# FAVOR+ attention followed by a gated MLP on one core: instruction order from an event-by-event model, tanh in place of silu, fewer DVE scalars and a second buffer for fetched weights

## Chip, core and metric

One core of one Trainium2 chip. The metric is the device time of one execution in microseconds (us); lower is better. A core has five instruction queues that run side by side, each strictly in its own order: PE (matrix multiply; its weight loads are shown as PEld), ACT (activation functions and copies), DVE (vector), POOL (a second vector engine) and SP (which here only issues DMA transfers). An instruction at the head of a queue that waits for data holds everything behind it on that queue.

## What is computed

```python
scale = D ** -0.25                                # 8 batches, 8 heads, 576 rows, D = 64
phi(x) = exp(x @ omega.T - sum(x*x)/2 - max) / sqrt(128)        # 128 features
q_p, k_p = phi(q * scale), phi(k * scale)
kv, z = k_p.T @ v, sum(k_p)                       # per batch and head
x = (q_p @ kv) / (q_p @ z + 1e-6)                 # 4608 x 512, heads side by side
g, val = x @ w_gate, x @ w_val                    # 512 x 1536 each
out = (g * sigmoid(g) * val) @ w_out              # 4608 x 512, float32
```

## The kernel before

**Attention.** The (batch, head pair, 256 rows) groups are walked in 72 steps (`NS`), two groups a step: first k groups alone, from step 6 a q group beside a k group, at the end q groups alone. Step n goes through these functions: `load` and `load_v` issue the loads of `nat` (q and k) and `v` on SP (L341, L348; `nat` has 3 buffers); `st_transpose` transposes on PE (`pt`, L383), squares on POOL (`sq`, L390) and copies to `x` on ACT (L391); `st_project` multiplies by omega (`pp`, L406); `st_max` reduces squares and maxima on DVE (L417 to L427) into a statistics tile `st`, the bias of the exponentials; `st_exp` makes the eight exponentials of the step on ACT (`ph`, L438); `k_accumulate` sums k features times v on PE (`kvacc`, L540) two steps later; `q_transpose`, `q_mult`, `q_out` and, for batches from 4 on, `q_den` and `q_norm` make x from the q features. The sums z of these later batches go through `kv_finalize`, which also transposes them on PE (L460) and writes them to DRAM, and `load_z`, which reads them back on all partitions.

**Weights.** The three weight matrices come in as 64-bit floats seen as pairs of 32-bit words. `convert_all` makes 36 pieces of 128x512 float32 out of them. One piece is: a 512 KB load (`st<-in_moe_w_...`, L232 or L237) into one of **two** staging buffers (`tag="stw"`; the trace calls this tile `st` too, but its lines tell it from the statistics), two ACT instructions (L268 and L276), three DVE instructions (L270, L272, L274), one POOL addition (L278), and a 256 KB write of the result to a scratch tensor (`wscr`, L281). The first nine pieces are also split at once into a high and a low part (`split_piece`: ACT L250, POOL L251). A staging buffer is free for the load of the piece after next when the POOL addition is done.

**MLP.** Float32 products are made of three matmuls of high and low parts. `stream` visits (512 tokens, three of the twelve weight slices): three times `g` (L657, 12 matmuls each), silu from PSUM to `sl` on ACT (L731), outstanding down projections (`o`, L666), three times `v` (L657), the product `sl` times `v` on DVE (L750), its split, and later the down projections. `g`, `v` and `o` share three PSUM buffers. The last four token tiles are done in pairs (`pair_rounds`): seven products instead of eight (`product`, L872), whose operands `make_seven` forms on DVE (L848 to L851) from weight pieces that `fetch` reads back into three `wraw` buffers (L306); there silu is in `gate` (L944).

**Order.** The Python loop at the end walks the steps and, in each, calls the functions in a fixed list (`CLOSE` while n < `EARLY`, then `GROUPED`), gives the MLP a share (`give`) and the conversion a number of ticks (`tick`) so that six pieces are due by step `EARLY` and the rest by later marks. What is traced earlier has priority. The order in which each queue finally holds its instructions is found afterwards by the library's scheduler: it plays the program through a model of the machine and gives every queue, whenever it comes free there, the ready instruction of highest priority. Silu and the exponential need different tables on ACT, and a table load stands before each change between them.

## Time and profile before

| | |
|---|---|
| three runs | 1203.81, 1209.05, 1226.72 us; median 1209.05 |
| the profiled execution | 1207.78 us; its span in the trace 1206.0 us |
| granted TensorE clock | 0.993 of full on average |
| PE idle in the span | 1206.0 - 1165.7 = 40.3 us |
| PE idle from 0 to 37 us | 9.95 us |
| PE idle from 37 to 130.3 us (attention only) | 4.25 us |
| PE idle from 130.3 to 452 us (attention and MLP) | 15.4 us |
| PE idle from 452 to 844 us | 1.3 us |
| PE idle from 844 to 876 us (first pair) | 4.5 us |

How to read it: a row of a group gives line, engine, operation, the tile written and those read, the count, then busy us, mean ns of one, and the idle time of the engine just before them with what ended it. A row of the timeline gives start us, length us, engine, line, operation and count; in square brackets stand idle time of the engine before it and what ended that. A row of the waits gives the waiting engine and line, what it waited for, total us, times, longest. Matmuls overlap, so a busy PE is not a PE at its peak: a matmul of 128x512 shows about 390 ns, but one follows the other 227 ns later.

### The profile page before, as it was taken

The numbers are of one execution on the slowest core, as the hardware profiler recorded it, in microseconds if no ns is written. First come the engines' busy times: TensorE is split into PE (matmuls) and PEld (weight loads), VectorE is DVE, ScalarE is ACT, GpSimd is POOL, SyncE is SP. The second block draws the span as 40 slices with busy tenths as digits, with TensorE's granted clock in tenths as the row PEclk, the third lists the DMA queues.
The fourth block names the chain that finished last, engine by engine and source line by source line (L and its number), as shares of the span: only waits on it lengthen the run. The fifth ranks groups of instructions, "written<-read, shape, count | busy, mean of one in ns | idle before, by whom it ended". The sixth has DMA issues, their size and how long they took to land.

```text
span 1206.0 us, 18814 instructions
## 1 busy us (share of the span) xinstructions
PE 1165.7 (97%) x6705; PEld 964.4 (80%) x6705; DVE 595.7 (49%) x1159; ACT 679.9 (56%) x1497; POOL 572.7 (47%) x500
## 2 busy tenths in 40 slices
PE   6999999999999999999999999999899999999998
PEld 5888787877887778888888787878688888888886
DVE  3687674345454644434332353373534556535544
ACT  4888977576566555556465656343454435454431
POOL 3333343334254546535445776344655543555541
PEclk9999999999999999999999999999999999999999
DMA  6555665344344423345222221334311111321103
GB/s 150 141 136 142 164 201 159 87 125 134 103 118 131 138 74 79 79 107 122 62 60 68 71 66 45 106 87 139 88 53 53 53 44 27 105 53 53 53 18 70
DMA packets 174110, 113.53 MB, mean 94 GB/s; under 512 B 125856, under 2 KB 144320, under 8 KB 174016
## 3 DMA queue, kind: packets, MB, share of 16 engines
q1 hardware_dynamic: 174016, 112.32, 34.9%
q8 instruction: 53, 0.87, 0.3%
q14 instruction: 41, 0.34, 0.1%
HBM read 87.10 MB, written 25.18 MB: 93 GB/s over the span
## 4 chain that ended last, share of the span: by engine, by line
PE 66%; DMA 4%; DVE 3%; POOL 3%; ACT 3%; issue 2%; SPq 1%; POOLq 0%; ACTq 0%; DVEq 0%
PE o L666 22%; PE a L872 10%; PE v L657 8%; PE g L657 8%; PE c L872 5%; PE pp L406 3%; PE d L872 2%; PE kvacc L540 2%; PE ptq L564 2%; PE xt L621 1%; PE pt L383 1%; POOL wlo L251 1%; DMA st<-in_moe_w_out_dram 1%; ACT ph L438 1%; DMA nat<-in_k_dram 1%
## 5 line engine op out<-in xcount | busy, mean ns | idle before, releaser
L438 ACT ACTIVATE ph<-pp,st 128x128 f32<-128x128 f32 x576 | 157.6, 389 | 17.0 <-DVE st L427 16.4
L695 DVE TENSOR_TENSOR acc<-o,acc 128x512 f32<-128x512 f32 x140 | 95.7, 685 | 104.7 <-PE o L666 104.7
L390 POOL TENSOR_TENSOR sq<-nat 128x512 f32<-128x512 f32 x72 | 75.6, 1051 | 146.0 <-DMA nat<-in_k_dram 116.9
L424 DVE TENSOR_REDUCE st<-pp 128x4 f32<-128x512 f32 x144 | 92.8, 683 | 72.5 <-PE pp L406 72.3
L251 POOL TENSOR_TENSOR wlo<-wraw,whi 128x512 fp32r<-128x512 f32 x76 | 99.9, 1324 | 55.3 <-ACT whi L250 55.1
L666 PE MATMUL o<-whi,hh 128*128 128x512 f32 x240 | 97.3, 406 | 3.1 <-ACT sl L731 3.0
L666 PE MATMUL o<-whi,hl 128*128 128x512 f32 x240 | 95.1, 396 | 1.2 <-POOL hl L754 1.2
L657 PE MATMUL g<-xh,whi 128*128 128x512 f32 x240 | 96.1, 400 | 0.0
L657 PE MATMUL v<-xh,whi 128*128 128x512 f32 x240 | 95.7, 399 | 0.2 <-DVE acc L695 0.2
L500 POOL TENSOR_TENSOR jk<-ph,zt 128x512 f32<-128x512 f32 x32 | 41.6, 1305 | 112.8 <-ACT ph L438 112.8
L666 PE MATMUL o<-wlo,hh 128*128 128x512 f32 x240 | 95.1, 396 | 0.0
L406 PE MATMUL pp<-omT,x 64*128 64x128 f32 x1152 | 92.8, 297 | 2.3 <-ACT x L391 2.2
L657 PE MATMUL g<-xh,wlo 128*128 128x512 f32 x240 | 94.0, 392 | 0.0
L657 PE MATMUL v<-xh,wlo 128*128 128x512 f32 x240 | 93.8, 391 | 0.0
L657 PE MATMUL g<-xl,whi 128*128 128x512 f32 x240 | 93.8, 391 | 0.0
L657 PE MATMUL v<-xl,whi 128*128 128x512 f32 x240 | 93.6, 390 | 0.0
L754 POOL TENSOR_TENSOR hl<-sl,hh 128x512 fp32r<-128x512 f32 x60 | 79.0, 1320 | 27.1 <-ACT hh L753 26.9
L406 PEld LDWEIGHTS pp<-omT,x 64*128 64x128 f32 x1152 | 76.0, 196 | 19.1 <-issue 11.6
L417 DVE TENSOR_REDUCE st<-sq 128x8 f32<-128x512 f32 x72 | 49.1, 681 | 85.5 <-POOL sq L390 85.4
L863 POOL TENSOR_TENSOR wlo<-s,whi 128x512 fp32r<-128x512 f32 x44 | 65.3, 1502 | 34.3 <-DVE late L969 11.8
L863 POOL TENSOR_TENSOR wlo<-wraw,whi 128x256 fp32r<-128x256 f32 (+1 forms) x44 | 45.2, 1026 | 74.9 <-ACT whi L862 74.7
L540 PE MATMUL kvacc<-v,ph 128*128 128x65 f32 x512 | 69.3, 277 | 3.4 <-ACT ph L438 3.4
(251 smaller groups left out, 2854.8 us busy)
## 6 DMA issues: line engine op xcount, KB each, us to landing
wraw<-wscr SPq DMA_DIRECT2D x120, 256.0 KB, 2.7
wscr<-wc SPq DMA_DIRECT2D x36, 256.0 KB, 2.4
out_dram<-acc SPq DMA_DIRECT2D x72, 128.0 KB, 2.3
nat<-in_k_dram SPq DMA_DIRECT2D x64, 128.0 KB, 3.1
v<-in_v_dram SPq DMA_DIRECT2D x64, 128.0 KB, 3.2
nat<-in_q_dram SPq DMA_DIRECT2D x64, 128.0 KB, 3.0
st<-in_moe_w_gate_dram SPq DMA_DIRECT2D x12, 512.0 KB, 5.2
st<-in_moe_w_val_dram SPq DMA_DIRECT2D x12, 512.0 KB, 4.6
```

Source lines behind the costliest of these rows:

```text
L251: nc.gpsimd.tensor_tensor(lo, raw, hi.bitcast(F32), op=ALU.subtract)
L390: nc.gpsimd.tensor_tensor(sq, nat, nat, op=ALU.mult)
L406: nc.tensor.matmul(pp[hh][:, i, c, :], x[r, i, c * P : (c + 1) * P], omT[r], start=True, stop=True)
L424: nc.vector.tensor_reduce(st[:, 1, :, :, hh], pp[hh], axis=AX.X, op=ALU.max, negate=True)
L438: nc.scalar.activation(ph[:, c, hh * M : (hh + 1) * M], pp[hh][:, i, c, :], AF.Exp, bias=st[:, 3, i, c, hh : hh + 1], scale=1.0,)
L540: nc.tensor.matmul(acc[:, 2 * (pr % 2) + hh, :], ph[:, c, hh * M : (hh + 1) * M], vt[:, 2 * c + j if gr is None else c, hh, :], start=firs ...
L657: nc.tensor.matmul(ps, a_[:, ws], b_[:, c, :], start=n == 0, stop=n == 3 * NC - 1)
L666: nc.tensor.matmul(ps, a_[:, ts_], b_, start=first and n == 0, stop=last and n == 2)
L695: nc.vector.tensor_tensor(a_, po, a_, op=ALU.add)
L754: nc.gpsimd.tensor_tensor(hl, h, hh.bitcast(F32), op=ALU.subtract)
L863: nc.gpsimd.tensor_tensor(lo, src_, hi.bitcast(F32), op=ALU.subtract)
L872: nc.tensor.matmul(ps, a_[:, w_], b_[:, c, :], start=start and c == 0 and m == 0, stop=c == CH - 1 and m == 2, skip_group_check=True,)
```

## The change

1. The whole kernel stands inside `tc.block(schedule_with_timeline_sim=True)`: the scheduler finds the order with a different model of the machine, an event-by-event one. No priority and no call is changed by this line.
2. `st_max` and `q_den`: sums with constants (`-SQC`, `EPS`) become reductions over a pair of columns, one of which a POOL memset has filled once. Per step that is three small reductions in place of two `scalar_tensor_tensor`; the statistics are six fixed tiles instead of six buffers of a pool.
3. `kv_finalize` no longer transposes the sums z; `z_rows` does, called first in each step's list (`GROUPED`), so one step later.
4. In `stream`, silu becomes tanh(g/2) on ACT, and (tanh + 1) times g on DVE, read from the same PSUM buffer (L750 of the changed file); the factor 0.5 goes into the product with `v`. In `gate` of the pairs, silu stays.
5. In the pairs, `fetch` for the next pair's first two weight kinds uses the five `first` buffers of the pool `win`, which are free by then, instead of the three `wraw` buffers.

```diff
+    ctx.enter_context(tc.block(schedule_with_timeline_sim=True))
     nc = tc.nc
...
-    def fetch(fs, i):
+    def fetch(fs, i, spare=None):
...
-            raw = moe.tile([P, DM], F32, name=f"wraw{f}_{i}", tag="wraw", bufs=3)
+            if spare is None:
+                raw = moe.tile([P, DM], F32, name=f"wraw{f}_{i}", tag="wraw", bufs=3)
+            else:
+                raw = spare.tile([P, DM], F32, name=f"wspare{f}_{i}", tag="first", bufs=5)
...
-        nc.vector.tensor_reduce(
-            st[:, 0].rearrange("p i c h -> p (i c h)"),
-            sq.rearrange("p i c h d -> p (i c h) d"),
-            axis=AX.X,
-            op=ALU.add,
-        )
+        nc.vector.tensor_reduce(st[:, :, 0], sq.rearrange("p i c h d -> p (i c h) d"), axis=AX.X, op=ALU.add)
+        nc.vector.tensor_reduce(st[:, :, 3], st[:, :, 0:2], axis=AX.X, op=ALU.mult)
...
-            nc.vector.tensor_reduce(st[:, 1, :, :, hh], pp[hh], axis=AX.X, op=ALU.max, negate=True)
-        s0, s1, s2, s3 = (st[:, j].rearrange("p i c h -> p (i c h)") for j in range(4))
-        nc.vector.scalar_tensor_tensor(s2, s0, SQC, s1, op0=ALU.mult, op1=ALU.add)
-        nc.vector.scalar_tensor_tensor(s3, s0, -SQC, s2, op0=ALU.mult, op1=ALU.add)
+            nc.vector.tensor_reduce(top[:, :, :, hh], pp[hh], axis=AX.X, op=ALU.max)
+        nc.vector.tensor_reduce(st[:, :, 4], st[:, :, 2:4], axis=AX.X, op=ALU.add, negate=True)
+        nc.vector.tensor_reduce(st[:, :, 5], st[:, :, 3:5], axis=AX.X, op=ALU.add)
...
+    def z_rows():
+
+        for (b, a2), raw in zraw.items():
             zp = ps_att(f"zp{b}_{a2}", [4, P])
             nc.tensor.transpose(zp, raw[:, :, D], ident)
...
-                nc.scalar.activation(sl, pg[f], AF.Silu)
+                nc.scalar.activation(sl, pg[f], AF.Tanh, scale=0.5)
+                nc.vector.scalar_tensor_tensor(sl, sl, 1.0, pg[f], op0=ALU.add, op1=ALU.mult)
...
-                nc.vector.tensor_tensor(h, pv, h, op=ALU.mult)
+                nc.vector.scalar_tensor_tensor(h, pv, 0.5, h, op0=ALU.mult, op1=ALU.mult)
...
-                        coming[i] = fetch((2 * pf2, 2 * pf2 + 1), i)
+                        coming[i] = fetch((2 * pf2, 2 * pf2 + 1), i, late_pools["win"])
...
     GROUPED = (
+        lambda n: z_rows(),
         q_out,
```

**What moves.** Three places, on the queues that the prediction is about. In the rows, the number after `ph`, `kvr` or `nat` that isn't its last is the step, the first number after `wc`, `whi` or a weight's `st` is the weight kind, and last numbers are only tile identities; `x2` is two instructions of one row.

The first is ACT at attention steps 5 and 6. Before:

```order
L391 COPY x_436<-pt_431 128x512
L438 ACTIVATE ph_5_454<-pp_5_420,st_382 128x128 x2
L438 ACTIVATE ph_5_454<-pp_5_421,st_382 128x128 x2
L438 ACTIVATE ph_5_459<-pp_5_420,st_382 128x128 x2
L438 ACTIVATE ph_5_459<-pp_5_421,st_382 128x128 x2
L391 COPY x_488<-pt_483 128x512
L454 COPY kvr_1_497<-kvacc_1_392 128x260
L268 ACTIVATE wc_0_595<-st_0_369 128x512
L438 ACTIVATE ph_6_509<-pp_6_471,st_437 128x128 x2
```

Now, the same engine from the last exponentials of step 4 on:

```order
L442 ACTIVATE ph_4_435<-pp_4_384,st_124 128x128 x2
L269 ACTIVATE wc_1_1183<-st_1_896 128x512
L277 ACTIVATE st_1_896<-st_1_896 128x512
L269 ACTIVATE wc_1_1473<-st_1_1179 128x512
L277 ACTIVATE st_1_1179<-st_1_1179 128x512
L251 CAST whi_1_1181<-wc_1_1183 128x512
L398 COPY x_460<-pt_455 128x512
L442 ACTIVATE ph_5_478<-pp_5_444,st_125 128x128 x2
L442 ACTIVATE ph_5_478<-pp_5_445,st_125 128x128 x2
L442 ACTIVATE ph_5_483<-pp_5_444,st_125 128x128 x2
L442 ACTIVATE ph_5_483<-pp_5_445,st_125 128x128 x2
L269 ACTIVATE wc_2_1885<-st_2_1469 128x512
```

Two pieces of the conversion (`wc`) now stand between the exponentials of one step and those of the next. Counting the first instructions of a piece (L268, now L269) ahead of each step's exponentials: before, 2 are ahead of step 4, 3 of step 9, 5 of step 15, 8 of step 24 and 19 of step 34; now 4 are ahead of step 4, then 6, 8, 10, 12 and 14 of steps 5 to 9, 19 of step 15, and still 19 of step 34. From step 36 on PE has the same counts of MLP and attention matmuls ahead of nearly every step as before.

The second is SP, which issues the loads. Before, at the loads of the fourth piece (`st_1_591`):

```order
L341 DMA nat_519<-in_q_dram 128x4x64
L341 DMA nat_519<-in_k_dram 128x4x64
L341 DMA v_101<-in_v_dram 128x4x64
L281 DMA wscr<-wc_0_373 128x512
L341 DMA nat_577<-in_q_dram 128x4x64
L341 DMA nat_577<-in_k_dram 128x4x64
L341 DMA v_102<-in_v_dram 128x4x64
L232 DMA st_1_591<-in_moe_w_val_dram 128x4x256
```

Now, at the loads of the sixth, seventh and eighth piece:

```order
L233 DMA st_1_1179<-in_moe_w_val_dram 128x4x256
L345 DMA v_102<-in_v_dram 128x4x64
L282 DMA wscr<-wc_1_1183 128x512
L238 DMA st_2_1469<-in_moe_w_out_dram 128x1024
L345 DMA nat_488<-in_q_dram 128x4x64
L345 DMA nat_488<-in_k_dram 128x4x64
L345 DMA v_103<-in_v_dram 128x4x64
L282 DMA wscr<-wc_1_1473 128x512
L345 DMA v_104<-in_v_dram 128x4x64
L238 DMA st_2_1881<-in_moe_w_out_dram 128x1024
```

Here a load of a piece and a write of a piece stand between the loads of every two attention steps, and each of them waits for the conversion of an earlier piece. Before, the loads of several steps stood between two of them.

The third is ACT at a visit of the MLP. Before, around the silus of one visit:

```order
L753 CAST hh_8_5358<-sl_8_5096 128x512
L731 ACT_TABLE_LOAD
L731 ACTIVATE sl_9_5473<-g_9_5368 128x512
L731 ACTIVATE sl_10_5475<-g_10_5382 128x512
L731 ACTIVATE sl_11_5477<-g_11_5395 128x512
L636 COPY xo_7_5_5418<-xt_7_5415 128x256
L566 COPY qt_8_5436<-ptq_8_5431 128x512
L391 COPY x_5468<-pt_5463 128x512
L438 ACT_TABLE_LOAD
```

Now:

```order
L772 CAST hh_8_5400<-sl_8_5133 128x512
L749 ACTIVATE sl_9_5514<-g_9_5410 128x512
L749 ACTIVATE sl_10_5517<-g_10_5424 128x512
L749 ACTIVATE sl_11_5520<-g_11_5437 128x512
L654 COPY xo_7_5_5460<-xt_7_5457 128x256
L584 COPY qt_8_5478<-ptq_8_5473 128x512
L442 ACTIVATE ph_52_5490<-pp_52_5463,st_124 128x128 x2
```

The two table loads around them are gone. In the whole program 58 of them stood on ACT and 2 are left: one at the start, and one at the first `gate` of the pairs.

## Prediction

> **What bounds the kernel now.** The page comes first, for the share of each engine.

> ```profile
> span 1206.0 us, 18814 instructions
> PE 1165.7 (97%) x6705; PEld 964.4 (80%) x6705; DVE 595.7 (49%) x1159; ACT 679.9 (56%) x1497; POOL 572.7 (47%) x500
> ```

> PE is the bound, idle for 40.3 us in all. What a new order can gain lies in those and in stretches where PE is busy but slow; what it can lose is open, so the next view is the table by stretches.

> ```profile
> 0.00:37.00 37.00, 27.05 (x156) 24.21 (x157) 15.19 (x33) 17.10 (x47) 14.53 (x31) 1.00 0.55 135
> 37.00:57.40 20.40, 19.25 (x197) 17.74 (x196) 14.32 (x33) 17.36 (x54) 7.34 (x7) 1.00 0.67 167
> 57.40:130.30 72.90, 69.80 (x663) 62.75 (x662) 56.59 (x152) 61.50 (x186) 26.20 (x24) 1.00 0.58 144
> 130.30:223.00 92.70, 88.61 (x615) 74.45 (x614) 51.84 (x127) 70.66 (x169) 32.17 (x29) 1.00 0.56 157
> 223.00:452.00 229.00, 217.67 (x1319) 179.42 (x1318) 113.45 (x221) 140.10 (x306) 102.35 (x86) 0.99 0.42 118
> 452.00:844.00 392.00, 390.66 (x2230) 315.81 (x2229) 160.33 (x307) 213.74 (x461) 205.85 (x180) 1.00 0.32 84
> 844.00:876.00 32.00, 27.47 (x106) 21.44 (x106) 18.65 (x30) 15.34 (x28) 18.95 (x15) 0.89 0.33 93
> ```

> The columns are the stretch, its length, busy us of PE, PEld, DVE, ACT and POOL, the granted clock, the DMA share and GB/s. From 37 to 130 us there is attention alone, and no engine is far from full: ACT 78.9 of 93.3 us, DVE 70.9, PE 89.1. From 130 us the MLP fills PE. From 452 us on PE waits for almost nothing, so an order has little to win there except at the first pair (844 to 876). The timeline then gives the pace of the attention, by the exponentials of steps 4, 5 and 9:

> ```profile
> 37.04 2.18 ACT L438 ACTIVATE ph<-pp,st 128x128 f32<-128x128 f32 x8 [0.83 <-DVE st L427]
> 40.81 2.18 ACT L438 ACTIVATE ph<-pp,st 128x128 f32<-128x128 f32 x8 [0.48 <-DVE st L427]
> ...
> 57.41 2.18 ACT L438 ACTIVATE ph<-pp,st 128x128 f32<-128x128 f32 x8
> ```

> Steps 4 to 9 take 57.4 - 37.0 = 20.4 us, 4.1 a step.

> **The change, part by part.** *The order of the conversion* is the largest term. The new order of ACT has two pieces ahead of the exponentials of each of the steps 5 to 9 (4 ahead of step 4, 14 ahead of step 9). ACT works in its order, so step n can't start its exponentials before two more pieces have been loaded. Loads go through two staging buffers, and piece k + 2 can only be loaded when piece k has gone through all of this:

> ```profile
> st<-in_moe_w_gate_dram SPq DMA_DIRECT2D x12, 512.0 KB, 5.2
> st<-in_moe_w_val_dram SPq DMA_DIRECT2D x12, 512.0 KB, 4.6
> st<-in_moe_w_out_dram SPq DMA_DIRECT2D x12, 512.0 KB, 3.8
> L268 ACT ACTIVATE wc<-st 128x512 f32<-128x512 f32 x36 | 24.3, 676 | 20.2 <-POOL wlo L251 6.0 <-DMA st<-in_moe_w_gate_dram 5.9 <-DMA st<-in_moe_w_out_dram 5.8
> L270 DVE TENSOR_SCALAR wc<-wc 128x512 f32<-128x512 f32 x36 | 23.4, 649 | 22.6 <-ACT wc L268 20.5 <-DMA wscr<-wc 2.0
> L272 DVE TENSOR_SCALAR wc<-wc 128x512 int32<-128x512 int32 x36 | 20.7, 577 | 0.5
> L274 DVE SCALAR_TENSOR_TENSOR st<-st,wc 128x512 int32<-128x512 int32 x36 | 27.0, 751 | 0.6
> L278 POOL TENSOR_TENSOR wc<-st 128x512 int32<-128x512 int32 x36 | 37.9, 1054 | 60.8 <-DVE st L274 15.3 <-ACT st L276 12.7 <-issue 11.9
> ```

> The mean landing of the three kinds is 4.5 us; with 0.68 on ACT, 0.65 + 0.58 + 0.75 on DVE and 1.05 on POOL that is 8.2 us, and with the write of the result issued ahead of the next load on SP (0.5 us, by the L281 rows below) 8.7. This is the floor of a round of two pieces. Waiting behind other work comes on top. How much, the nearest rows tell: where the kernel before converts as fast as it can, the loads into one of the two buffers follow each other like this.

> ```profile
> 148.73 0.57 SPq L237 DMA_DIRECT2D st<-in_moe_w_out_dram  x1
> ...
> 158.43 0.39 SPq L232 DMA_DIRECT2D st<-in_moe_w_val_dram  x1
> ...
> 168.59 0.58 SPq L281 DMA_DIRECT2D wscr<-wc  x1
> 169.28 0.39 SPq L232 DMA_DIRECT2D st<-in_moe_w_gate_dram  x1
> ...
> 178.36 0.33 SPq L281 DMA_DIRECT2D wscr<-wc  x1
> 178.87 0.33 SPq L237 DMA_DIRECT2D st<-in_moe_w_out_dram  x1
> ```

> That is 9.7, 10.9 and 9.6 us: 10.1 a round. In the changed order the exponentials (2.18) stand between the pieces of a round on ACT, and the loads of `nat` and `v` between those of the pieces on SP, so I take 10.2. Steps 4 to 9 are five rounds, 51 us, against 20.4: **+31**. The exponentials of step 4 already stand behind two pieces more than before and behind their splits, which wait for POOL; I estimate **+3** for that. Bounds: five rounds at the floor, 43.5 us, give +23 and nothing before; rounds of 11.5 give +37, and +5 before, 42. Nothing covers this delay: the MLP can't begin before step 25 of the attention has given its first tokens, and behind the waiting piece on ACT stand the exponentials, behind those the sums of k features on PE; on SP, the loads of later steps. From step 9 to 15 five more pieces, two and a half rounds or 25.5 us, stand against 28.8 us (57.41 to 86.24) that these steps took: no further delay.

> ```profile
> 86.24 2.18 ACT L438 ACTIVATE ph<-pp,st 128x128 f32<-128x128 f32 x8 [0.39 <-DVE st L427]
> ```

> *What that gives back.* Steps 16 to 24 lose 3 pieces, each about 1.4 us on ACT (two instructions like L268) and 2.0 on DVE; PE has 3.1 us idle from 57 to 130 us in all: **-3**, between 0 and -5. Steps 25 to 34 lose all of their eleven pieces; PE is idle there for 4.1 us, with short gaps in its busy time of about as much (an estimate): **-5**, between -2 and -8.

> *The table loads.* 56 of 58 go; a load is 1.28 us:

> ```profile
> L731 ACT ACT_TABLE_LOAD x29 | 37.2, 1283 | 1.7 <-PE g L657 1.1
> L438 ACT ACT_TABLE_LOAD x28 | 35.9, 1283 | 0.5
> ```

> They are 72 us of ACT, but ACT is at 140 of 229 us where PE still waits (223 to 452), and at 214 of 392 where it hardly does. What PE pays is seen at its longest wait there:

> ```profile
> 406.85 0.67 ACT L268 ACTIVATE wc<-st 128x512 f32<-128x512 f32 x1 [1.28 <-DMA st<-in_moe_w_val_dram]
> 407.41 2.17 ACT L438 ACTIVATE ph<-pp,st 128x128 f32<-128x128 f32 x8
> 409.60 1.28 ACT L731 ACT_TABLE_LOAD   x1
> 410.89 0.60 ACT L731 ACTIVATE sl<-g 128x512 f32<-128x512 f32 x1
> 411.54 0.52 PE L666 MATMUL o<-whi,hh 128*128 128x512 f32 x1 [2.99 <-ACT sl L731]
> ```

> Of 2.99 us the table load is 1.28; the rest is a piece of the conversion waiting for its load, which the new order still has at this place. So of the 11.3 us idle from 223 to 452 I take not quite half: **-5**, between 0 and -11. [...]

> *Tanh* takes ACT what silu took, I assume; the added operation on DVE is bounded below by nothing and above by the like product, 0.69 us:

> ```profile
> L750 DVE TENSOR_TENSOR sl<-v,sl 128x512 f32<-128x512 f32 x60 | 40.9, 685 | 40.4 <-PE v L657 40.1
> ```

> 60 of them are 41 us for a DVE that is half idle. A PSUM buffer comes free later by these 0.7 us and what DVE does first, but the buffer of the first of three `g` is only wanted after two more (24 matmuls of 0.227 us, 5.4 us): 0; if that cover is gone, it is in a rival below. The third small reduction per step is off the path from maximum to exponential, which still has two: 0. *The z sums*: PE waited for them once, by the row here: **-1**, between 0 and -2.

> ```profile
> PE zp L460 <- ACT kvr L454: 1.1, 1, 1.1
> ```

> *The fetch of the pairs* ends a chain of late operands:

> ```profile
> DVE s L848 <- DMA wraw<-wscr: 56.9, 10, 7.2
> PE a L872 <- DVE sl2k L969: 3.2, 1, 3.2
> ```

> From 844 to 876 PE is idle for 4.5 us, and the granted clock is 0.89, which is another (1 - 0.89) x 32 = 3.5. With two more buffers the fetch is issued before the old pieces are split: **-5**, between 0 and -7.

> Sum: 31 + 3 - 3 - 5 - 5 - 1 - 5 = **+15**. On the profiled execution, 1207.8 us (its span and 1.8 around it), that is **1223 us**; that execution lies 1.3 us below the median of the runs shown. With the bounds of the terms: 23 - 33 = -10 or 1198, and 42 - 2 = +40 or 1248; all ends at once is unlikely.

> **The rivals.** *Not slower: the delay is repaid.* The early pieces cost their floor (+23), and every stall that ACT or DVE causes afterwards goes: -3, -8, -11, -1, -7, together -30. Sum -7, about **1200 us**. For it speaks that table loads and fourteen pieces are 72 + 20 us less of ACT after step 15, and that DMA is at 0.55 to 0.67 early, so landings needn't get worse. Against it: the longest wait of PE in the middle, quoted above, begins with a piece of the conversion whose place hasn't moved. It decides when the round is near 8.7 and not 10.2. Chance 0.25, and a third of that below 1185.

> *Slower by over 2%: PE stays slow.* PE runs at half speed at first:

> ```profile
> 27.74 2.08 PE L406 MATMUL pp<-omT,x 64*128 64x128 f32 x16
> 41.31 1.16 PE L406 MATMUL pp<-omT,x 64*128 64x128 f32 x16
> ```

> The same sixteen matmuls take 2.08 and, from 38 us on, 1.16. If PE, now with pauses between steps, stays slow to step 15, a step's work there, 4.7 us at full speed (69.8 us busy for the 15 steps from 9 to 24), is some 8 us if most of it doubles, instead of the 4.8 that a step from 9 to 15 takes: six steps by 3.2, +19, so **1242 us**. It decides if the clock rises only under denser work than two pieces a step leave. [...] Later freed PSUM buffers (20 visits by up to 1.4 us, 28) would end on the same side, at 1251. Together 0.20.

> *The order does nothing on the chip*, since other waits pace the early steps anyway: then the small terms alone remain, -11 to -14, **1195 us**. The 4.1 us steps speak against it. Chance 0.05.

> **How the numbers follow.** The forecast, 1223 us, has 0.50 with its own range 1208 to 1238. The range over all cases is 1194 to 1245. Two per cent, about what a measurement of this kernel can tell from no change, are 24 us about 1209: below 1185 or above 1233. Faster: a third of the first rival, with a little of the last, 0.10. Slower: 0.08 of the forecast's own upper end and 0.19 of the second rival, 0.27. Within: 0.63.

> **What would show it.** Right: exponentials of step 9 near 90 us instead of 57, those of step 15 near 120, ACT idle before L269 with the load of a piece behind it, and stretches from 250 us on nearly as before but for the table loads and the first pair. Wrong: step 9 before 75 us, or rounds of the staging buffers under 8 us; a first MLP matmul before 150 us; PE waits on `g` or `o` that end with the new operation on DVE.

## The result, and the profile after

The changed kernel takes **1266.63 us** (median of 4 runs, 1259.32 to 1269.54) against 1208.62 us of the kernel before on the same chip: ratio 1.046, 95% interval 1.042 to 1.050. It is slower by over 2%, and 44 us above the forecast. The profiled execution took 1268.14 us. Its page begins like this.

```profile
span 1266.4 us, 18952 instructions
PE 1209.0 (95%) x6705; PEld 998.6 (79%) x6705; DVE 664.6 (52%) x1291; ACT 606.9 (48%) x1441; POOL 579.8 (46%) x512
```

The span grew by 60.4 us. PE runs the same 6705 instructions, was idle for 1266.4 - 1209.0 = 57.4 us instead of 40.3, and was *busy* for 43.3 us longer. So only 17 of the 60 us are waits of PE; the rest is the same instructions taking longer. The table by stretches, cut at the same events (exponentials of steps 4, 9 and 15, first MLP matmul, exponentials of steps 26 and 34, then 452 us and the first pair), says where. Of the kernel after:

```profile
0.00:41.60 41.60, 24.70 (x156) 21.34 (x156) 21.06 (x48) 20.23 (x53) 19.69 (x47) 0.86 0.70 183
41.60:89.60 48.00, 32.91 (x211) 30.81 (x212) 28.86 (x65) 29.73 (x77) 22.02 (x20) 0.64 0.75 209
89.60:122.10 32.50, 29.78 (x248) 26.71 (x247) 22.95 (x63) 25.28 (x75) 11.16 (x11) 0.82 0.72 192
122.10:174.70 52.60, 47.00 (x361) 42.01 (x359) 31.41 (x87) 32.52 (x103) 10.62 (x11) 0.84 0.43 109
174.70:228.70 54.00, 49.82 (x270) 40.52 (x269) 18.20 (x50) 16.06 (x43) 5.94 (x5) 0.94 0.06 14
228.70:304.00 75.30, 72.17 (x478) 61.61 (x477) 29.88 (x86) 36.55 (x107) 13.46 (x13) 0.91 0.20 46
304.00:452.00 148.00, 146.86 (x890) 121.57 (x889) 87.81 (x178) 79.28 (x205) 67.05 (x56) 1.00 0.47 133
875.50:1266.00 390.50, 384.31 (x1693) 317.19 (x1691) 223.94 (x314) 172.98 (x302) 203.36 (x158) 1.00 0.22 62
```

Of the kernel before, the stretches from step 9 to 15, from there to the first MLP matmul (129.4 us), and from the first pair on:

```profile
57.40:86.20 28.80, 28.24 (x269) 25.62 (x267) 23.44 (x61) 24.65 (x74) 11.30 (x10) 1.00 0.52 127
86.20:129.40 43.20, 40.66 (x394) 36.36 (x390) 32.49 (x90) 36.18 (x110) 14.59 (x14) 1.00 0.63 157
825.20:1206.00 380.80, 371.47 (x1621) 305.54 (x1620) 192.12 (x300) 168.15 (x295) 193.54 (x153) 0.99 0.22 60
```

The reader is to see the granted clock, the third figure from the right. Before, it is 1.00 from 37 us to the first MLP matmul. After, it is 0.64, 0.82 and 0.84 there. (The clock records begin at 36.4 us before and at 23.0 us after; what lies ahead of them counts as full in these figures, so the first stretch can't be compared by them.) From 41.6 to 89.6 us PE is both idle for 15 us and granted only 0.64 of its clock. (In the half-clock record from 203.9 us on, matmuls of 128x512 follow each other after 0.42 us; at full clock, at 186 us, after 0.23.) The first MLP matmul comes 45.3 us later; the remaining 15.1 us are lost behind it.

How the early steps came to wait is what the prediction described: the timeline of ACT ahead of step 9, and that of the loads.

```profile
82.95 0.72 ACT L277 ACTIVATE st<-st 128x512 int32<-128x512 uint32 x1
87.24 0.66 ACT L269 ACTIVATE wc<-st 128x512 f32<-128x512 f32 x1 [3.57 <-DMA st<-in_moe_w_val_dram]
87.81 0.65 ACT L277 ACTIVATE st<-st 128x512 int32<-128x512 uint32 x1
88.36 0.35 ACT L660 CAST xh<-xt 128x256 fp32r<-128x256 f32 x1
88.62 0.59 ACT L398 COPY x<-pt 128x512 f32<-128x512 f32 x1
89.09 0.60 ACT L584 COPY qt<-ptq 128x512 f32<-128x512 f32 x1
89.57 0.65 ACT L442 ACTIVATE ph<-pp,st 128x128 f32<-128x128 f32 x2
```

```profile
43.56 0.38 SPq L233 DMA_DIRECT2D st<-in_moe_w_val_dram  x1
...
53.77 0.58 SPq L238 DMA_DIRECT2D st<-in_moe_w_out_dram  x1
...
63.78 0.60 SPq L233 DMA_DIRECT2D st<-in_moe_w_gate_dram  x1
...
73.91 0.37 SPq L238 DMA_DIRECT2D st<-in_moe_w_out_dram  x1
...
82.56 0.54 SPq L233 DMA_DIRECT2D st<-in_moe_w_val_dram  x1
```

ACT stands 3.57 us before L269, and behind that piece stand the copy of `x` (L398) that PE needs and the exponentials of step 9 (89.57). Loads into one staging buffer follow each other after 10.2, 10.0, 10.1 and 8.7 us. From 37 to 90 us ACT waits six times at L269, 15.9 us in all:

```profile
ACT wc L269 <- issue: 7.9, 3, 2.9
ACT wc L269 <- DMA v<-in_v_dram: 4.4, 2, 2.6
ACT wc L269 <- DMA st<-in_moe_w_val_dram: 3.6, 1, 3.6
```

Only the longest of the six is put down to the load of a piece; that the others wait for a piece too is inferred from the rounds of the loads. PE pays at the projections (view of waits, 0 to 90 us):

```profile
PE pp L413 <- ACT x L398: 18.3, 7, 5.9
```

### The profile page after: what moved, and what is told of

It reads as the page before. It is cut to its first block, busy times and chain, and to the rows that moved or that the text cites. A ratio compares the mean times of both kernels' runs of the same rounds, so it can differ in the third digit from the quotient of the medians.

```text
span 1266.4 us, 18952 instructions
## 1 busy us (share of the span) xinstructions
PE 1209.0 (95%) x6705; PEld 998.6 (79%) x6705; DVE 664.6 (52%) x1291; ACT 606.9 (48%) x1441; POOL 579.8 (46%) x512
## 4 chain that ended last, share of the span: by engine, by line
PE 82%; DVE 5%; ACT 4%; DMA 3%; issue 1%; POOL 0%; SPq 0%; ACTq 0%; POOLq 0%; DVEq 0%
PE o L684 22%; PE g L675 12%; PE v L675 12%; PE a L891 10%; PE pp L413 5%; PE c L891 5%; PE kvacc L558 4%; PE d L891 3%; PE ptq L582 2%; PE pt L390 2%; PE xt L639 2%; PE po L599 2%; ACT ph L442 2%; DMA nat<-in_k_dram 1%; DMA st<-in_moe_w_val_dram 1%
## 5 line engine op out<-in xcount | busy, mean ns | idle before, releaser
L397 POOL TENSOR_TENSOR sq<-nat 128x512 f32<-128x512 f32 x72 | 75.9, 1054 | 199.8 <-DMA nat<-in_k_dram 168.4
L252 POOL TENSOR_TENSOR wlo<-wraw,whi 128x512 fp32r<-128x512 f32 x76 | 104.2, 1381 | 56.8 <-ACT whi L251 56.6
L413 PE MATMUL pp<-omT,x 64*128 64x128 f32 x1152 | 108.7, 315 | 19.9 <-ACT x L398 19.2
L413 PEld LDWEIGHTS pp<-omT,x 64*128 64x128 f32 x1152 | 89.2, 212 | 42.0 <-ACT x L398 21.0
L428 DVE TENSOR_REDUCE st<-pp 128x4 f32<-128x512 f32 x144 | 93.3, 685 | 40.4 <-PE pp L413 40.0
L675 PE MATMUL g<-xh,wlo 128*128 128x512 f32 x240 | 96.7, 403 | 0.0
L675 PE MATMUL g<-xl,whi 128*128 128x512 f32 x240 | 96.6, 403 | 0.0
L675 PE MATMUL v<-xl,whi 128*128 128x512 f32 x240 | 94.1, 392 | 0.0
L882 POOL TENSOR_TENSOR wlo<-s,whi 128x512 fp32r<-128x512 f32 x44 | 60.6, 1379 | 56.2 <-ACT whi L881 50.7
L423 DVE TENSOR_REDUCE st<-sq 128x8 f32<-128x512 f32 x72 | 49.3, 684 | 68.1 <-POOL sq L397 68.0
L558 PE MATMUL kvacc<-v,ph 128*128 128x65 f32 x512 | 79.4, 300 | 4.4 <-ACT kvr L458 4.1
L558 PEld LDWEIGHTS kvacc<-v,ph 128*128 128x128 f32 x512 | 74.1, 218 | 8.8 <-ACT kvr L458 4.3
L517 POOL TENSOR_TENSOR jk<-ph,zt 128x512 f32<-128x512 f32 x32 | 41.2, 1294 | 85.8 <-ACT ph L442 85.6
## 6 DMA issues: line engine op xcount, KB each, us to landing
st<-in_moe_w_gate_dram SPq DMA_DIRECT2D x12, 512.0 KB, 5.0
```

Of the source, the lines that this page charges most:

```text
L252: nc.gpsimd.tensor_tensor(lo, raw, hi.bitcast(F32), op=ALU.subtract)
L397: nc.gpsimd.tensor_tensor(sq, nat, nat, op=ALU.mult)
L413: nc.tensor.matmul(pp[hh][:, i, c, :], x[r, i, c * P : (c + 1) * P], omT[r], start=True, stop=True)
L428: nc.vector.tensor_reduce(top[:, :, :, hh], pp[hh], axis=AX.X, op=ALU.max)
L558: nc.tensor.matmul(acc[:, 2 * (pr % 2) + hh, :], ph[:, c, hh * M : (hh + 1) * M], vt[:, 2 * c + j if gr is None else c, hh, :], start=firs ...
L675: nc.tensor.matmul(ps, a_[:, ws], b_[:, c, :], start=n == 0, stop=n == 3 * NC - 1)
```

## The experiments

**Theory A**, the prediction's: the pieces that the order pulls ahead of the exponentials on ACT are the loss. **Theory B**: the block's order of the attention and the MLP loses by itself, wherever the pieces stand. **Theory C** came from the profiles, when neither A nor B had fitted all runs: single pauses of PE send its clock to half, so that a pause is paid again in slower work. (In the expectations of `e1_block_only` and `e2_no_block`, which are older, "Theory C" means another thing: that the other edits lose the time.) The table has all runs; "step 9" is when that step's exponentials begin, "first MLP" the first MLP matmul, and "idle" is span less busy time of PE on the page. Each ratio, with its 95% interval, is to the kernel before in the same series of runs, which has 1205.0 to 1209.5 us in the five series.

| kernel | median us | ratio to before | step 9 | first MLP | span | PE busy | idle |
|---|---|---|---|---|---|---|---|
| before | 1208.6 | | 57.4 | 129.4 | 1206.0 | 1165.7 | 40.3 |
| after | 1266.6 | 1.046 [1.042, 1.050] | 89.6 | 174.7 | 1266.4 | 1209.0 | 57.4 |
| e1_block_only | 1268.7 | 1.050 [1.042, 1.058] | 89.5 | 172.7 | 1265.1 | 1207.1 | 58.0 |
| e2_no_block | 1225.0 | 1.013 [1.006, 1.021] | 51.3 | 123.7 | 1218.9 | 1166.6 | 52.3 |
| e6_early_conv | 1254.3 | 1.038 [1.031, 1.045] | 84.6 | 167.7 | 1253.0 | 1184.9 | 68.1 |
| e4_tied | 1264.9 | 1.047 [1.040, 1.054] | 74.4 | 172.5 | 1268.7 | 1220.4 | 48.3 |
| e9_act_tied | 1249.9 | 1.038 [1.035, 1.042] | 70.8 | 155.2 | 1246.5 | 1198.8 | 47.7 |
| e10_pe_tied | 1260.9 | 1.048 [1.044, 1.052] | 88.6 | 171.0 | 1256.6 | 1199.3 | 57.3 |
| e11_both_tied | 1266.6 | 1.051 [1.046, 1.055] | 70.0 | 165.2 | 1266.5 | 1211.1 | 55.4 |
| e7_no_spare | 1212.9 | 1.007 [1.005, 1.010] | 51.4 | 123.3 | 1205.5 | 1160.4 | 45.1 |
| e8_sums_z | 1205.7 | 0.998 [0.995, 1.001] | 51.9 | 122.8 | 1204.7 | 1163.5 | 41.2 |
| p0_order | 1363.1 | 1.131 [1.126, 1.135] | 64.1 | 194.1 | 1358.9 | 1218.3 | 140.6 |
| p1_pause | 1369.3 | 1.136 [1.131, 1.140] | 73.3 | 201.1 | 1370.6 | 1231.3 | 139.3 |
| p2_filled | 1379.9 | 1.144 [1.139, 1.149] | 80.5 | 219.6 | 1386.2 | 1250.0 | 136.2 |
| q1_short | 1299.1 | 1.075 [1.065, 1.085] | 56.9 | 128.5 | 1294.9 | 1200.8 | 94.1 |
| q2_long | 1253.9 | 1.036 [1.028, 1.045] | 53.3 | 124.7 | 1254.0 | 1178.8 | 75.2 |
| e16_filled | 1273.6 | 1.051 [1.041, 1.061] | 87.5 | 193.6 | 1275.2 | 1228.4 | 46.8 |

### The block alone, and all but the block

`e1_block_only` is the kernel before with one line more, `e2_no_block` the changed kernel without that line:

```diff
+    ctx.enter_context(tc.block(schedule_with_timeline_sim=True))
```

> The kernel before with the one line of the block and nothing else of the change. Theory A (the new order loses the time, first of all by the weight pieces pulled ahead of the attention steps): 1255 to 1280 us, exponentials of step 9 near 90 us and of step 15 near 122. Theory C (the other edits, tanh or the z sums or the fetch, lose it): within 10 us of the kernel before.

> The changed kernel without the line of the block: sums, z rows, tanh and the fetch buffers of the pairs in the standard order. Theory A: 1190 to 1208 us, so faster than before by what the prediction summed for the small terms (1 to 14 us), and exponentials of step 9 near 57 us. Theory C: 1250 us or more.

The block alone is the whole result: 1.050 against 1.046. Without it the other edits bring the first MLP matmul forward by 5.7 us, but the run is 1.3% slower than before instead of faster. Both facts matter below: the order loses the 60 us, and the other edits don't win where the trace of before said that they would.

### The pieces pulled ahead, in the old order

`e6_early_conv` takes the block away and moves the pieces by the program's own table of marks, so that 13 stand ahead of step 9 and 19 ahead of step 15; PE keeps the old order.

```diff
-    marks = [(0, 0.0), (EARLY, 2 * FA), (EARLY + 2, 3 * FA)]
-    for k_ in range(1, NSET):
+    marks = [(0, 0.0), (3, 5), (8, 15), (14, 19), (34, 19)]
+    for k_ in range(2, NSET):
```

> The kernel of the run without the block, with the marks of the conversion moved so that 13 pieces stand ahead of step 9 and 19 ahead of step 15, in the standard order. Theory A: exponentials of step 9 at 80 to 95 us, of step 15 at 110 to 125, total 20 to 40 us above the run without the block. Theory B: within 10 us of it.

Against `e2_no_block` the first MLP matmul comes 44.0 us later and the run takes 29 us more (34 in the profiled executions); so behind it the early pieces give some 10 us back (in the spans, 1085.3 us instead of 1095.2). The delay is shown outside the block, for A. But here too PE is slow: its clock from 0 to 84.6 us is 0.70, where it was 0.96.

```profile
0.00:84.60 84.60, 71.51 (x673) 65.15 (x673) 54.38 (x154) 62.71 (x188) 34.24 (x61) 0.96 0.64 155
```

```profile
0.00:84.60 84.60, 58.66 (x368) 52.40 (x368) 51.60 (x104) 49.40 (x128) 37.77 (x62) 0.70 0.65 177
```

The first of these rows is of `e2_no_block`, the second of `e6_early_conv`.

### The pieces held back, inside the block

`e4_tied` queues each piece's load behind the last attention load written so far; `e9_act_tied` queues each piece's first operation on ACT behind the last exponential.

```diff
 # e4_tied
+                with tc.issue_after(last_load[0].ins):
                     nc.sync.dma_start(raw, ...)
 # e9_act_tied
+                with tc.issue_after(last_exp[0].ins):
                     nc.scalar.activation(u, r, AF.Abs)
```

> The changed kernel, with each load of a weight piece queued on SP behind the last attention load traced before it, so that pieces can't run ahead of the program; 5 instead of 14 are then ahead of step 9 on ACT, and PE keeps the order of the changed kernel (122 MLP matmuls ahead of step 26). Theory A, the pieces alone: exponentials of step 9 near 60 us, of step 15 near 90, total 1215 to 1232 us. Theory B (the order of PE from step 16 on, and with it the slow clock, loses most): step 9 early, but a total of 1245 us or more.

> The changed kernel, with the first operation of every weight piece on ACT put behind the last exponential that the program has written so far; the block may order all the rest. In its order 3 pieces stand ahead of the exponentials of step 9 and 6 ahead of those of step 25 (changed kernel: 14 and 19). Theory A (the pieces pulled ahead of the exponentials on ACT are the whole loss before the MLP): exponentials of step 9 at 50 to 62 us, first MLP matmul at 115 to 135 instead of 175, median 1215 to 1232, since the some 15 us that the block loses after the first MLP matmul stay. Theory B (the block loses by its order on PE, and the pieces only fill the waits): first MLP matmul not before 155, median 1245 or more.

Both missed what A expects, and both came out as B expects. In `e4_tied` steps 4 to 9 take 36.2 us instead of 48.0, but with PE busy nearly all the time at a clock of 0.55, and by the first MLP matmul all is lost again: PE's idle time is 9 us less than after, its busy time 11 us more.

```profile
38.20:74.40 36.20, 34.52 (x203) 32.79 (x203) 16.70 (x42) 18.92 (x57) 11.10 (x11) 0.55 0.45 114
```

In `e9_act_tied` the pieces stand where the program has them (3 ahead of step 9), which gives back some 10 us (1.038 against 1.046), and the first MLP matmul still comes at 155.2. The table by windows of 3.41 us, laid on the edges at which the clock records change, shows what is left:

```profile
118.37:121.79 3.42, 3.19 (x27) 2.76 (x27) 2.18 (x9) 1.65 (x5) 1.18 (x2) 1.00 0.34 77
121.79:125.20 3.41, 1.28 (x22) 0.92 (x20) 1.62 (x5) 2.38 (x9) 0.46 (x1) 1.00 0.34 77
125.20:128.61 3.41, 3.41 (x18) 3.41 (x17) 1.30 (x4) 1.95 (x7) 1.89 (x2) 0.50 0.42 95
128.61:132.03 3.42, 3.42 (x18) 3.30 (x19) 2.54 (x6) 1.65 (x6) 1.23 (x2) 0.50 0.21 49
132.03:135.44 3.41, 3.41 (x24) 3.19 (x24) 1.46 (x4) 1.06 (x2) 1.27 (x1) 0.50 0.84 256
135.44:138.85 3.41, 3.41 (x24) 3.21 (x23) 0.94 (x4) 1.76 (x6) 0.00 (x0) 0.50 0.12 32
138.85:142.27 3.42, 3.42 (x19) 3.28 (x17) 2.06 (x5) 2.91 (x11) 0.00 (x0) 0.50 0.08 17
142.27:145.68 3.41, 3.41 (x30) 3.22 (x30) 1.05 (x4) 2.24 (x7) 0.00 (x0) 1.00 0.17 38
```

In the second window PE works for 1.28 of 3.41 us (pauses of 1.9 and 0.2 us), and the next five are at half clock though PE is busy for all of them: idle time of 2.1 us is followed by 17.1 us in which up to 8.5 us of work are lost. That is theory C.

### The MLP's early run on PE

In the block's order 122 MLP matmuls stand ahead of the projection of step 26, and lagged work on q features between them; before it were 30. `e10_pe_tied` queues the MLP's matmuls behind the last projection written so far (24 ahead), and `e11_both_tied` does this and what `e9_act_tied` does.

```diff
+                with tc.issue_after(last_pp[0].ins):
                     nc.tensor.matmul(ps, a_[:, ws], b_[:, c, :], ...)
```

> The changed kernel, with every matmul of the MLP put behind the last projection matmul that the program has written so far, so that the MLP can't run ahead of the attention on PE; the pieces of weights stay ahead of the exponentials (14 before step 9). 24 MLP matmuls stand ahead of the projection of step 26 instead of 122. Theory A: no change up to the first MLP matmul (170 to 180 us); then the projections of steps 25 and 26 come 10 to 15 us apart instead of 47, and the median is 1250 to 1260. If the MLP's early run on PE was also what made the rest slow, 1240 or less; if its order costs nothing, 1262 to 1270. Theory B: 1225 or less.

> The changed kernel with both ties: weight pieces behind the exponentials, MLP matmuls behind the projections, as the program writes them. Theory A: the two together are the loss of the block, so 1205 to 1222, at or under the change without its block (1225). Theory B, or a third part of the order (transposes, sums of k and of q) that costs by itself: 1235 or more.

The first gives back nothing that can be told from noise (1.048 against 1.046 and 1.050). The projections of its steps 25 and 26 are still 33.6 us apart, not 10 to 15, with 24 us of half clock from 181.5 us on. The second gives back nothing either, against what A expects of it: with both ties PE's clock from step 15 to the first MLP matmul is 0.69, and that stretch, 98.1 to 165.2 us, is longer than in any other run with the block. So no single part of the order that I tied is the loss. A fits `e6_early_conv` but not `e4_tied`, `e9_act_tied` and `e11_both_tied`; B fits these three but not `e6_early_conv`. What all these slow orders have in common is half clock at changing places: from the exponentials of step 4 to the first MLP matmul the records show 63 us of it after, 40 to 87 us in the five other runs with the block so far, 41 in `e6_early_conv`, and none in the kernel before or in `e2_no_block`.

### What a pause of PE costs

`p0_order` is the kernel before in the order in which the program is written, on all engines. `p1_pause` puts five copies on ACT ahead of `x` in four steps, and `p2_filled` fills these pauses with matmuls whose results are overwritten.

```diff
+        if n in (8, 12, 16, 20):
+            for _ in range(5):
+                nc.scalar.copy(x, pt)
         nc.scalar.copy(x, pt)
```

> The kernel before, with every instruction queued behind the one written before it on its engine (all five engines), so that nothing is reordered: the base for the next two, which add instructions and move none. 1200 to 1240 expected; no theory hangs on its level.

> p0_order with five more copies of the same tile on ACT (about 2.9 us) ahead of x in the steps 8, 12, 16 and 20; all else in the same order. Theory C (a pause of PE of some 2 us, about half of a window of 3.4 us, sends the next one to five windows to half clock, so that it is paid twice or more): records of half clock of 12 to 40 us in all between steps 8 and 25 that p0_order doesn't have, and 17 to 35 us more than p0_order, though the pauses themselves are 4 x 2.9 = 11.6. Rival (the clock follows the mean load over tens of us and not one pause): no more than 4 us of half clock, and 12 us more or less than that.

> p1_pause with forty more matmuls of omT with itself on PE (2.3 to 2.9 us at full clock) ahead of the projections of those four steps, whose results the projections overwrite: PE has as many pauses to wait through but works in them. Theory C: no half clock there, and at most 12 us more than p0_order, 6 to 25 less than p1_pause. Rival: as p1_pause or up to 12 us above it, since the extra matmuls come on top.

Both speak for the rival. By their totals, `p1_pause` is 6 us above `p0_order`, and the filled one 11 more. By the clock records, from step 8 to step 25 `p0_order` has 69 us of half clock, `p1_pause` 66 and `p2_filled` 79, where C expects 12 to 40 us more in the second and fewer in the third. They are a poor test all the same, since the base is not what I took it for. Written order costs 13%, and PE's clock is 0.75 from step 9 to 20 in `p0_order` already:

```profile
64.10:154.40 90.30, 67.84 (x485) 61.27 (x487) 39.73 (x107) 44.77 (x133) 18.24 (x17) 0.75 0.29 75
```

The next two put pauses into the stage of the pairs of the kernel before, where PE has hardly a gap: a small matmul, copies of its result on ACT, a small matmul on the copy, and the next product queued behind it. `q1_short` has 42 pauses of three copies, `q2_long` 6 of sixteen.

```diff
+        with tc.issue_after(tail[0].ins):
+            nc.tensor.matmul(t[:, 0:P], ident, ident, start=True, stop=True)
+        for _ in range(COPIES):
+            nc.scalar.copy(scr, t[:, 0:P])
+        tail[0] = nc.tensor.matmul(t[:, 0:P], ident, scr, start=True, stop=True)
```

> The kernel before with 42 short pauses of PE in the stage of the pairs, where PE is otherwise without a gap: before every fourth product a small matmul, three copies of its result on ACT one after the other (0.27 us each) and a small matmul on that copy, behind which the next product is queued. About 1.1 to 1.4 us each, 46 to 59 us in all, over some 400 us. Theory C (the clock falls for the window after one in which PE was busy for less than about 0.6 of 3.4 us): a window holds one such pause and is busy for two thirds, so no more than 10 us of half clock, and the run is longer by the pauses themselves, 45 to 62 us. Rival (the clock follows the mean load, however the idle time is cut): as many us of half clock for each us idle as in the next run, or more, since more is idle.

> The same with 6 long pauses, before every 28th product with sixteen copies: about 4.6 us each, 28 us in all. Theory C: each is followed by one to three windows at half clock, 20 to 50 us of half clock beyond the kernel before, and the run is longer by the pauses and half of that, 38 to 53 us. Rival: 26 to 31 us and no more half clock than in the kernel before.

The windows around the second long pause (of `q2_long`), and one with a short pause and its next (of `q1_short`):

```profile
953.95:957.37 3.42, 0.11 (x1) 0.00 (x0) 0.93 (x2) 2.81 (x10) 3.42 (x3) 1.00 0.00 0
957.37:960.78 3.41, 1.17 (x4) 1.07 (x5) 0.00 (x0) 1.97 (x8) 0.48 (x1) 0.50 0.00 0
960.78:964.20 3.42, 3.42 (x10) 2.65 (x9) 0.69 (x1) 0.40 (x1) 0.74 (x1) 0.50 0.00 0
964.20:967.60 3.40, 3.40 (x17) 2.79 (x16) 0.69 (x1) 2.25 (x4) 2.62 (x3) 1.00 0.44 93
```

```profile
926.50:929.90 3.40, 1.99 (x11) 1.61 (x10) 1.98 (x3) 1.31 (x4) 1.64 (x2) 1.00 0.25 80
929.90:933.30 3.40, 3.40 (x17) 2.80 (x16) 1.94 (x2) 1.25 (x2) 1.50 (x3) 1.00 0.02 5
```

Each of the six long pauses (5.6 to 6.5 us of idle PE) brings 6.8 us of half clock; the 42 short ones (1.0 to 3.1 us, half of them under 1.41) 17 us in all, where the kernel before has 9 from the first pair on. In us of half clock for each us of added idle time (53.8 and 34.9 us) that is 0.15 against 1.0: in these two runs the length of the single pause decided, not the idle share, as C says. `q2_long` cost what C expected (46 us in the medians). `q1_short` didn't: 91 us instead of 45 to 62. Its idle time is within that range; but PE's busy time grew by 35 us too. Its small matmuls, each of which goes as two instructions (`x2` in its timeline at 927.63 and 929.42 us), keep PE busy for 30 of them by the trace, and half clock accounts for about the rest.

`e16_filled` puts twelve more matmuls ahead of the projections of steps 3 to 24 of `e9_act_tied`.

> The run with weight pieces behind the exponentials (block, 1250) and twelve more matmuls of omT with itself ahead of the projections of each step from 3 to 24, whose results are overwritten: 22 x 0.8 = 18 us of work for PE that nothing needs. Theory C: it fills windows that were sparse, so that the half clock from step 4 to the first MLP matmul falls from 40 us to under 20, and the run is within 1238 to 1252 in spite of the added work. Rival (the clock isn't what costs): 1258 to 1270.

C missed here. The total lies above even the rival's range, and from step 4 to the first MLP matmul the half clock falls from 40 us to 36 only, not to under 20. PE was busy for 30 us more, not 18 (two instructions for each matmul again), and the added work moved the block's order, so the total doesn't decide. Only in one part of the stretch, from step 15 to the first MLP matmul, does the filling do what C says. The first row is of `e9_act_tied`, the second of `e16_filled`: 231 matmul instructions more, in 2.5 us more, at 0.97 instead of 0.82.

```profile
97.80:155.20 57.40, 50.30 (x385) 45.24 (x385) 31.86 (x93) 35.03 (x108) 15.11 (x14) 0.82 0.38 95
```

```profile
133.70:193.60 59.90, 57.16 (x616) 51.37 (x614) 32.99 (x95) 36.33 (x108) 13.84 (x13) 0.97 0.35 88
```

### The other edits, without the block

`e7_no_spare` is `e2_no_block` with the old buffers for the fetch of the pairs; `e8_sums_z` has silu again as well, so that only the sums and z sums remain.

> The change without the block and without the new fetch buffers of the pairs (sums, z sums and tanh remain). If the two late stalls of the pairs in the run without the block (PE waiting some 3 us each for ACT behind VectorE's seven sums) come from the earlier fetch: they are gone, the stretch from the first pair on is as before, and the median is 1212 to 1218. If they come from tanh or the sums: 1222 to 1230.

> The kernel before with the new sums and z sums alone: no block, silu as before, no new fetch buffers. The run with tanh beside it was 0.7% slower than before. If that loss is tanh's (an operation more on DVE in front of the normalization of the attention, PE waiting for xn and xo between 225 and 450 us): 1195 to 1206, the version that beats both. If it is that of the sums: 1208 to 1216.

The fetch buffers cost outside the block. With them PE has two stalls of 3.1 us in the pairs behind a late copy on ACT, which waits for VectorE; the stage takes 388.9 us instead of 379.4 in the profiled executions. In the medians the two, of different series, aren't clear of noise: 1.013 [1.006, 1.021] against 1.007 [1.005, 1.010]. The wait, and one of VectorE's groups from 890 to 1100 us (in the kernel `e2_no_block`):

```profile
PE a L890 <- ACT late L983: 6.3, 2, 3.1
```

```profile
L866 DVE TENSOR_TENSOR s<-wspare 128x256 f32<-128x256 f32 x12 | 11.6, 965 | 12.5 <-POOL wlo L881 12.5
```

What is earlier there is the seven sums of a visit (L866 to L869), which the old buffers had held back. The sums alone are no different from the kernel before (0.998), the best of all versions and no measurable gain. Tanh beside them is 0.7% slower than before, in another series; the two profiled executions differ by 0.8 us only, so where tanh's part goes stays open.

## Why the prediction was wrong, point by point

**The step that failed: the sum counts waits of PE and has nothing for slower work.** But for small shares of two terms (short gaps in steps 25 to 34, 3.5 us of clock at the first pair), its terms are waits of PE. Their sum was +15, and PE's idle time grew by 17.1 us. What the sum left at nothing is PE's busy time, and that grew by 43.3 us with the same 6705 instructions. In time, +31 was forecast up to the first MLP matmul and 45.3 us were measured; behind it -16 was forecast and +15.1 measured. So two thirds of the miss lie behind the first MLP matmul.

**That the waits came out so near is in part luck.** Up to the first MLP matmul the terms are +31 + 3 - 3 = +31; the rows give 174.7 - 134.4 = 40.3 us idle against 129.4 - 115.2 = 14.2, so +26. Behind it -16 was predicted and -9 measured. The two errors cancel.

*The order of the conversion, +31.* Steps 4 to 9 took 48.0 us against 20.4: +27.6, in rounds of 9.8 us on the mean instead of 10.2. Step 9's exponentials came at 89.6, as predicted "near 90". The delay was right; but only 13.9 us of it are idle time of PE, and 13.7 are busy time, at a clock of 0.64.

*Step 4, +3:* 41.6 against 37.0, +4.6.

*Steps 9 to 15, no further delay.* Wrong by a little: 32.5 us against 28.8, with PE at 0.82 and idle for 2.7 us. Step 15 came at 122.1.

*Steps 16 to 24, -3.* This is the first term with the wrong sign. From step 15 to the first MLP matmul no piece was to be converted any more, and ACT has 32.5 us of work in 52.6. But the stretch took 9.4 us longer than before instead of 3 less, at a clock of 0.84 instead of 1.00. "No conversions" took the load off ACT and DVE, which were not what set the pace there.

*Steps 25 to 34 (-5) and the table loads (-5).* The waits they stood for did go in the block: PE is idle for 1.1 us from 304 to 452. Outside it they didn't: `e2_no_block`, which has 2 table loads, is idle for 16.1 us from its step 34 to 452 us, the kernel before for 11.3. And from the first MLP matmul to the end the kernel takes 1091.7 us, 15.1 more than before: PE is idle for 9 us less there and busy for 24 more. In the first 54 us of it SP had issued next to nothing (DMA 0.06), ACT has 16 us of work, and PE runs 122 MLP matmuls and lagged attention work ahead of step 26. `e10_pe_tied` takes most of this early run away and is no faster, so it isn't shown to be the cost.

*The z sums, -1:* no wait of PE for them is left. As predicted.

*The pairs, -5:* in the block 390.5 us, with 72 matmul instructions of the last MLP visit in it (16.3 us at 0.227 each), so 374.2 against 380.8, -6.6. The size is right by luck, for the fetch buffers didn't bring it: `e1_block_only`, which has the old ones, takes 390.2 us for the same stage (874.9 to 1265.1), with 1694 matmul instructions against 1693. Outside the block the same edit costs 9.5 in the profiled executions.

*Tanh's operation on DVE, 0:* PE's waits from 300 us on that end with it (L750) are 0.4 us in all. As predicted in the block; outside it the 0.7% of `e7_no_spare` stay open.

**The rival that was nearest had part of the mechanism.** "PE stays slow" had 0.20 and 1242 us: the forecast and 19 us of slow work, in steps 9 to 15 alone, for a clock that has not risen yet. Those steps took 3.7 us more. What the trace shows is a clock that rises and falls back again and again up to the first MLP matmul. How much of PE's busy time this makes follows from the rows: the clock lacks 0.36, 0.18 and 0.16 over 48.0, 32.5 and 52.6 us, together 31.5 us, and PE is busy for 82% of that time: 26 us. That is not yet time of the kernel: some 12 of it lie in steps 4 to 9, where the rounds of the pieces would give the delay without it. Of the other 17 us of the 43, some 5 are half clock behind the first MLP matmul (24.8 us of records against 15.8 before). The rest is work at full clock. Behind the first MLP matmul, at full clock, PE goes from one kind of matmul (by the tile written) to another 778 times, in the kernel before 653 times (776 in `e1_block_only`, 634 in `e2_no_block`); that could be the rest, but no run tests it.

The rival was said to decide "if the clock rises only under denser work than two pieces a step leave". In the rows of `e9_act_tied` above, half clock followed on a single window with PE busy for 1.28 of 3.41 us; full clock came back not after one busy window but after the fifth.

What is shown: the block's line alone makes the loss; early pieces cost 44 us up to the first MLP matmul in the old order too; each long pause of `q2_long` (5.6 to 6.5 us) was followed by half clock, and a short one of `q1_short` (1.0 to 3.1 us) mostly was not. What is only worked out: that 26 us of PE's longer busy time are half clock. What is not shown: how much of the 60 us the half clock makes, since the runs that fill pauses (`p2_filled`, `e16_filled`) didn't get shorter. Which part of the order would have to change to avoid the pauses stays open; three ties didn't find it.

## What to carry to other kernels

Look at PE's busy time before its idle time: if the same instructions were busy for 43 us longer, the waits explain the smaller part of a loss. On a stretch where PE is just about dense, set a new wait against the 3.41 us by which the clock changed in these records: a window of that length less than half filled was followed by half clock 144 times of 151 here, and what that costs varies, from some 2 us after each long pause of `q2_long` to up to 8.5 us after the 2.1 us of `e9_act_tied`. An order that fills ACT's waits with work of another stage can cost PE more in busy time than in waits: 43 us against 17 here. And a term that comes out right needs a run without the edit that it stands for: the pairs got faster in the block with the old buffers too.

## What the runs showed of the hardware

I hadn't expected written order to cost 13% (1363 us): the reordering that the kernel before gets without a block is worth more than all edits here.
